# Query and key products of the second layer: three of four blocks as seven products on sums of pairs of weight tiles, with the sums made at the end of the first gated stage

## The chip, the core and the metric

The kernel runs on one core of a Trainium2 chip. The metric is the device time of one execution in microseconds (us); the time before is the median of three executions, 1891.64 us (1891.1 to 1893.27). The engines are named as in the profile: PE (TensorE matmul), PEld (its weight loads), DVE (VectorE), ACT (ScalarE), POOL (GpSimd) and SP (SyncE); POOL and SP issue most of the DMAs here, each in its program's order.

## The reference

Two layers, each an attention block and a gated block, with the same weights in both layers. S = 2048 tokens, D = 448, H = 16 heads of 28, F = 1792.

```python
def _A_ref(x, wqkv, wo):
    qkv = ((x @ wqkv).reshape(B, S, 3, H, Dh)).transpose(2, 0, 3, 1, 4)
    q, k, v = qkv[0], qkv[1], qkv[2]
    scores = jnp.einsum("bhqd,bhkd->bhqk", q, k) * (Dh ** -0.5)
    o = jnp.einsum("bhqk,bhkd->bhqd", softmax(scores), v)
    return o.transpose(0, 2, 1, 3).reshape(B, S, D) @ wo
def _B_ref(x, w_gate, w_up, w_down):
    return (sigmoid(x @ w_gate) * (x @ w_up)) @ w_down

x = x + _A_ref(layernorm(x), wqkv, wo)
x = x + _B_ref(layernorm(x), w_gate, w_up, w_down)
x = x + _A_ref(layernorm(x), wqkv, wo)
x = x + _B_ref(layernorm(x), w_gate, w_up, w_down)
```

## The kernel before

The tokens lie in 16 tiles of 128, worked on in four blocks of 512 (`NB = 4`, `W = 512`). All inputs of the matrix products are split into a high and a low float16 part, and three of the four part products are summed in PSUM (high by high, low by high, high by low). D = 448 is three tiles of 128 and a tail of 64; the tail's high and low parts share one tile.

Instructions stand on each engine in the order in which the code emits them (`tc.manual_schedule()`); there is no scheduler. SBUF is dealt out by two pools of slots, `big` (19 slots) and `qrt` (12): `get` takes the slot that has been free longest, `put` appends to the free list, and whoever writes a slot next waits for its last readers.

A layer is `project` (query, key and value products), `attend`, `out_project` and `gated`.

**project.** `qk(b, blk, fill, before)` makes the 896 query and key rows of one block as seven tiles of 128 rows. Each tile is one PSUM bank, 128 x 512, filled by `by_features` with 11 matmuls 512 wide (nine for the three whole tiles, two for the tail). ACT turns the bank into a high part (L765), DVE into a low part (L766), ACT squares (L768), DVE takes maxima of the squares (L772), the SP queue stores both parts in `qk_scr` (L775), and small matmuls (L744, L747) collect the squares of a head, three tiles late. `fill` holds work for the next block, done after the tile of that index. `vals` follows with four tiles of values of 11 matmuls 448 wide each (L587 to L592). After the last block, `guard_of_norms` pops the last collected norms (`fin`), loads the first heads, and bounds the scores; `attend` starts when the first score operands have landed.

**gated.** Gate and up products are already in the seven-product form, on pairs (128 x 256 quarters) of a weight pair: `of_halves` emits six 256-wide matmuls for the products 0 to 3 (operands `wide`) and five for 4 to 6 (operands `short`), and `gate_and_up` spreads the seven over a `chain` bank, which ACT copies out after each product, and a `side` bank, which DVE adds up. The sums of the weight tiles come from `Prepare`, which makes them once during the first layer's attention, with DVE alone, in float16 parts (`N_SUMS = 25` tiles of 128 x 128 a pair).

The down products lag one block behind: while block b does its gate and up products, `pieces` does the down products of block b - 1, one of the seven operand sets `dn` for each of the seven pairs p. After the last block a tail remains: the seven down products of block 3, in the order `TAIL = (0, 1, 3, 2, 5, 4, 6)`. The first three are run for six pairs each, then each is finished with the seventh pair; the other four follow whole, 42 matmuls of 224 columns each. `finish(b, k)` adds a bank to x on DVE (L1596), and products 2, 5 and 4 go on accumulating in the bank that the first three left, after that addition. `used_dn` gives the operand slot back and issues the load of the next operand set on the POOL queue, always three ahead:

```python
def used_dn(self):
    (big.put_next if self.pairs else big.put)(self.dn.popleft())
    if self.products:
        self.load_dn(nc.gpsimd)
```

During the last block of the first layer's gated stage, `steps` also holds the work for the first two blocks of the next layer (norms on DVE and POOL, `lift` on ACT, `square` on DVE, stores and gathers on SP), dealt out by `portions(b, p)`; and with the last pair `wq.load` brings the query, key and value parts back from `qk_parts` and `v_parts`, where the first layer had left them (`keep`).

Of the kernel before, what the change touches and what calls it, by code (L numbers as in the profile page):

```python
# [16 lines left out]
ALU = mybir.AluOpType  # L17
# [53 lines left out]
TAIL = (0, 1, 3, 2, 5, 4, 6)  # L71

# [46 lines left out]
def interleaved_layers(ctx: ExitStack, tc: tile.TileContext, x_in, wqkv, wo, w_gate, w_up,  # L119
# [122 lines left out]

    def powers(c, n, squares):
# [20 lines left out]
    class Block:  # L264
# [10 lines left out]
        def __init__(self, b, halves=False):  # L275
            self.b = b
            self.halves = halves
            self.turned = False
# [107 lines left out]
        def half_steps(self):  # L386
# [43 lines left out]
            def r11():  # L430
                self.wide = big.get("xwide", [P, 4, 2, 2, W // 2], F16)
                self.short = big.get("xshort", [P, 3, 2, 2, W // 2], F16)
# [36 lines left out]

            def last_low():  # L470
                low(self.short[:, 2], cut(2, 2))
# [7 lines left out]
            return [r11, t1, t2, t3, r21, t4, r22, last_low, last_rows]  # L479
# [121 lines left out]
    class WeightsQKV:  # L601
# [65 lines left out]

        def load(self):
            self.tiles()
            for i in range(2):  # L670
                nc.sync.dma_start(self.qk[i], qk_parts[i])
            nc.sync.dma_start(self.v, v_parts)

# [46 lines left out]
    def project(layer, wq, begun):  # L720
# [68 lines left out]

        def values_product(pv, blk, j, kts=range(4)):  # L790
            t = slice(j * P, (j + 1) * P)
            by_tokens(pv[:, 0:D], lambda kt: blk.hi[:, kt, t], lambda kt: blk.lo[:, kt, t],
                      blk.tail[:, t], wq.v, kts)

        def vals(b, blk, after, tiles=range(TB), at=None, begun=None):
            for j in tiles:
                pv = begun or bank(evac[0] % 4 if at is None else at, "vp")
                evac[0] += 1
# [31 lines left out]
        blks = begun + [Block(b) for b in range(len(begun), NB)]  # L830
# [3 lines left out]
        if layer == 0:  # L834
# [5 lines left out]
            def turned(kts):  # L840
                b1.turn_banks(6, kts)
                for j in range(TB):
# [9 lines left out]
                            3: lambda: (b2.squares(), b2.store(), tell.read())}  # L852
        else:
            ones_of_values()
            fill = [idle, lambda: b1.ready(0, 1), lambda: b1.ready(2, 3), b2.norm,
                    lambda: b2.squares([0, 1]), sq(2, 2, 3), b2.store]
            along_values = {0: b3.norm, 1: sq(3, 0, 1), 2: lambda: (fin(), b2.gather()),
                            3: sq(3, 2, 3)}
        fin = qk(0, blks[0], fill, None)
        vals(0, blks[0], along_values)  # L860
        if layer == 0:
            fill = [b2.gather, b3.norm, sq(3, 0, 1), sq(3, 2, 3), idle,
                    lambda: b2.ready(0, 1), lambda: (b2.ready(2, 3), b3.store())]
        else:
            fill = [idle, lambda: b2.ready(0, 1), lambda: b2.ready(2, 3), b3.store]
        fin = qk(1, b1, fill, None)
        vals(1, b1, {0: b3.gather, 2 if layer == 0 else 1: fin})
        add = tell.add if layer == 0 else idle
        fin = qk(2, b2, [idle, lambda: b3.ready(0, 1), lambda: b3.ready(2, 3), idle, add, add,
                         add], None)  # L870
        fin = qk(3, blks[3], [add, add, add], fin)
        if layer > 0:
            big.put(*wq.qk)
# [34 lines left out]
        vals(2, blks[2], {0: guard_of_norms, 3: worst_of_heads})  # L908
# [15 lines left out]
        def last_values(begun=None):  # L924
# [6 lines left out]
            if layer > 0:  # L931
                big.put(wq.v)
# [72 lines left out]
    class Prepare:  # L1005
# [86 lines left out]
        def add_up(self, v):  # L1092

            s12, s34 = [qrt.get("sums", [P, 2, 2, P]) for _ in range(2)]
            l11, l12, l21, l22 = v[:, 0:2, 0], v[:, 2:4, 0], v[:, 0:2, 1], v[:, 2:4, 1]
            for to, a, b, op in ((s12[:, 0], l21, l22, ALU.add),
                                 (s12[:, 1], s12[:, 0], l11, ALU.subtract),
                                 (s34[:, 0], l11, l21, ALU.subtract),
                                 (s34[:, 1], l12, s12[:, 1], ALU.subtract)):
                nc.vector.tensor_tensor(to, a, b, op=op)  # L1100
            return s12, s34

# [22 lines left out]
        def split(self, raw, kind, j):  # L1125
# [5 lines left out]
            elif kind in "gu":  # L1131
                m = "gu".index(kind)
                t = big.at(self.packs, "pack", [P, N_SUMS, P], F16)
                sums = self.add_up(v)
                s12, s34 = [a.rearrange("p a k n -> p (a k) n") for a in sums]
                for to, a in ((t[:, 0:2], v[:, 0:2, 0]), (t[:, 2:6], s12), (t[:, 6:10], s34),
                              (t[:, 10:14].rearrange("p (k z) n -> p k z n", k=2), v[:, 2:4])):
                    scaled_high(to, a, 4 + m, nc.vector)
                for to, hi, a in ((t[:, 14:16], t[:, 0:2], v[:, 0:2, 0]),
                                  (t[:, 16:20], t[:, 2:6], s12),  # L1140
                                  (t[:, 20:23], t[:, 6:9], s34[:, 0:3]),
                                  (t[:, 23:25], t[:, 10:12], v[:, 2])):
                    scaled_low(to, hi, a, 4 + m)
                scaled_low(t[64:P, 9], t[0:64, 9], s34[0:64, 3], 4 + m)
                scaled_low(t[64:P, 12:14], t[0:64, 12:14], v[0:64, 3], 4 + m)
# [785 lines left out]
```

## Time and profile before

| what | value |
|---|---|
| median of three executions | 1891.64 us |
| the profiled execution: time, and its span | 1891.53 us, 1889.8 us |
| PE, PEld busy | 1881.4 us (100%), 1334.4 us (71%) |
| DVE, ACT, POOL busy | 1444.7 us (76%), 1390.5 us (74%), 233.2 us (12%) |
| matmuls | 24,321 |
| DMA | 272 MB, mean 144 GB/s |
| first layer's gated stage, last down products (L1578) | 923.26 to 952.6 us |
| second layer's query, key and value products | 952.6 to 1052.7 us |
| the first of them: block 0 | query and key from 952.59, values from 969.49 us |

Times are counted from the start of the span. The time of an execution is 1.73 us longer than its span in the profiled run. A matmul's duration in the records includes its way through the array, which overlaps the next one; the step from one matmul to the next is read from two rows' starts divided by the matmuls between. In a timeline row, `x44` is the count of merged instructions, and a bracket gives the idle time of the engine ahead of it and what ended that.

### The profile page before, as it was taken

The page shows a single profiled execution, that of the slowest core. Times are in us where ns is not written, and L with a number is a line of the kernel's source. Part 1 is how long each engine was busy: PE and PEld are TensorE (multiplying, and loading weights), DVE is VectorE, ACT ScalarE, POOL GpSimd, SP SyncE. Part 2 cuts the span into 40 slices and gives each one's busy share as a digit, 9 for nine tenths or more (in the row PEclk, how much of TensorE's full clock was granted, in tenths as well). Part 3 has the DMA queues.
Part 4 walks back from the last instruction along what each step waited for, and adds up shares of the span by engine and source line. Part 5 has one row for each costly group of instructions (what it writes and reads, how often), then busy time and mean ns, then how long its engine had stood idle before and what let it go on. Part 6 is the DMA issues. An engine that isn't in the chain of part 4 may idle for free. (4 is left out here: it accounts for less than half of the span.)

```text
span 1889.8 us, 56477 instructions
## 1 busy us (share of the span) xinstructions
PE 1881.4 (100%) x24321; PEld 1334.4 (71%) x24321; DVE 1444.7 (76%) x2894; ACT 1390.5 (74%) x1793; POOL 233.2 (12%) x450
## 2 busy tenths in 40 slices
PE   9999999999999999999999999999999999999999
PEld 4455555556566899999954556766666568999998
DVE  7758989898977887787575487787778688877664
ACT  5569999999993655555345799999999747555541
POOL 3023112222102111111100000000000021111110
PEclk9999999999999999999999999999999999999999
DMA  7676444334323755646734322122120246566553
GB/s 247 194 217 162 133 132 128 106 121 132 101 89 93 261 207 208 228 180 243 251 97 134 90 52 50 30 52 52 30 49 21 72 160 234 200 227 223 207 207 142
DMA packets 109059, 272.01 MB, mean 144 GB/s; under 512 B 12958, under 2 KB 65566, under 8 KB 108672
## 3 DMA queue, kind: packets, MB, share of 16 engines
q0 software_dynamic: 32256, 160.12, 23.4%
q1 hardware_dynamic: 75392, 106.82, 19.8%
q8 instruction: 192, 3.15, 0.7%
q10 hardware_dynamic: 1152, 1.38, 0.3%
q14 instruction: 67, 0.55, 0.1%
HBM read 209.26 MB, written 50.62 MB: 138 GB/s over the span
## 5 line engine op out<-in xcount | busy, mean ns | idle before, releaser
L1233 ACT ACTIVATE prob_s<-sc 128x1536 f32<-128x1536 f32 (+1 forms) x657 | 888.0, 1485 | 7.3 <-DMA qp_s<-qk_scr 5.2
L1269 PE MATMUL acc<-prob_s,val_s 128*32 128x256 f32 (+3 forms) x7700 | 572.1, 384 | 0.0
L1218 PE MATMUL sc<-qp_s 114*32 114x512 f16 x7868 | 555.1, 379 | 0.0
L580 PEld LDWEIGHTS <-gu_s 128*128 128x128 f16 x4368 | 426.7, 98 | 46.1 <-PE op L1398 0.7
L1218 PEld LDWEIGHTS <-qp_s 114*32 114x32 f16 x8192 | 276.8, 95 | 200.4 <-issue 84.6
L1269 PEld LDWEIGHTS acc<-prob_s,val_s 128*32 128x32 f32 x7700 | 276.5, 110 | 139.7 <-issue 13.6
L580 PE MATMUL chain<-xwide_s,gu_s 128*128 128x256 f16 x2016 | 247.5, 273 | 0.1
L1578 PE MATMUL dnp<-dn_s,hparts_s 128*128 128x224 f16 x2184 | 245.9, 259 | 0.0
L1578 PEld LDWEIGHTS <-hparts_s 128*128 128x128 f16 x2184 | 210.2, 98 | 5.1
L1249 DVE SCALAR_TENSOR_TENSOR power_q<-power_q,expo_q 128x512 f32<-128x512 f32 x243 | 168.2, 692 | 8.3
L1651 ACT COPY one_q<-chain 128x256 f32<-128x256 f32 x224 | 82.4, 371 | 116.0 <-PE chain L580 115.5
L1667 DVE TENSOR_TENSOR one_q<-side,one_q 128x512 f32<-128x512 f32 x112 | 72.2, 686 | 99.0 <-PE side L580 98.6
L580 PE MATMUL side<-xshort_s,gu_s 128*128 128x256 f16 x1120 | 140.6, 273 | 0.0
L565 PE MATMUL qkp<-xhl_s,wqk_s 128*128 128x512 f16 x616 | 137.5, 379 | 0.9 <-ACT wqk_s L232 0.6
L1459 POOL DMA_DIRECT2D gu_s<-gu_parts x104 | 56.3, 541 | 428.4 <-PE side L580 424.9
L565 PEld LDWEIGHTS <-wqk_s 128*128 128x128 f16 x616 | 59.3, 98 | 70.1 <-ACT wqk_s L232 1.4
L1531 ACT CAST hparts_s<-hsums_q 128x256 f16<-128x256 f32 (+1 forms) x152 | 71.5, 485 | 37.1 <-DVE hsums_q L1543 23.4
L1298 DVE STREAM_TRANSPOSE oturned_q<-acc 128x512 f32<-128x512 f32 x32 | 22.9, 716 | 98.1 <-PE acc L1269 97.9
L1269 PE MATMUL acc<-power_q,val_s 128*32 128x256 f32 (+3 forms) x300 | 94.2, 396 | 0.0
L580 PE MATMUL side<-xwide_s,gu_s 128*128 128x256 f16 x672 | 91.7, 273 | 0.0
L765 ACT ACTIVATE qkhl_q<-qkp 128x512 f16<-128x512 f32 x56 | 33.2, 592 | 70.0 <-PE qkp L565 69.5
L1678 ACT ACTIVATE one_q<-one_q 128x512 f32<-128x512 f32 x56 | 35.3, 630 | 65.5 <-DVE one_q L1667 65.3
(215 smaller groups left out, 2283.8 us busy)
## 6 DMA issues: line engine op xcount, KB each, us to landing
gu_s<-gu_parts POOLq DMA_DIRECT2D x104, 800.0 KB, 5.9
dn_s<-dn_parts POOLq DMA_DIRECT2D x42, 784.0 KB, 7.5
qp_s<-qk_scr SPq DMA_DIRECT2D x96, 224.0 KB
qk_scr<-qkhl_q SPq DMA_DIRECT2D x56, 256.0 KB
gu_parts<-pack_s POOLq DMA_DIRECT2D x14, 800.0 KB, 3.8
xt_scr<-xs_s SPq DMA_DIRECT2D x48, 224.0 KB
xraw_s<-xt_scr SPq DMA_DIRECT2D x12, 768.0 KB
qp_s<-qk_scr SPq DMA_DIRECT2D x64, 112.0 KB
```

Of the source, the lines that this page charges most:

```text
L565: nc.tensor.matmul(pm, w, x, start=(i == 0), stop=(i == len(terms) - 1))
L580: nc.tensor.matmul(pm, a, x, start=(first and i == 0), stop=(i == len(terms) - 1), skip_group_check=True)
L1218: nc.tensor.matmul(ps[32 * j:32 * j + 32, :], hd.k[:, keys], hd.q[:, qb * W:(qb + 1) * W], start=True, stop=True, tile_position=(0, 32 * j))
L1233: nc.scalar.activation(prob[:, 0:n, :], ps[:, 0:n, :], AF.Exp, scale=exp_scale)
L1249: nc.vector.scalar_tensor_tensor(p, p, c[k], y, op0=ALU.add, op1=ALU.mult)
L1269: nc.tensor.matmul(acc[qb * VC:(qb + 1) * VC, s], v[:, kc % TB, h, :], probs[c * NB + qb][:, s], start=(kc == 0 and a == 0), stop=(kc == N ...
L1459: queue.dma_start(self.gu[-1][m], gu_parts[p, m])
L1531: nc.scalar.copy(to[:, :, 0], a)
L1578: nc.tensor.matmul(pm, a[:, x, t], w[:, p, y], start=(begin and n == 0 and (j == 0 or alone)), stop=(n == 2), skip_group_check=True)
L1651: nc.scalar.copy(to, pm)
L1667: nc.vector.tensor_tensor(one[m], side[m], one[m], op=ALU.add)
L1678: nc.scalar.activation(out, v, AF.Sigmoid, scale=gate_scale)
```

## The change

In the second layer, blocks 0, 2 and 3 no longer use `qk` but `qk_sums`; block 1 keeps `qk`. The seven row tiles are taken as three pairs, (0, 1), (4, 5), (2, 6), each in the seven-product form, and tile 3 alone in the usual form on 256-wide halves. A block then has 3 x 39 + 22 = 139 matmuls 256 wide in place of 77 matmuls 512 wide, and 16 norm matmuls 64 wide in place of 8 that are 128 wide. Each pair adds four ACT copies out of a chain bank and two DVE additions of a side bank, as in `gate_and_up`, ahead of the high, low and square steps of each tile. The operands of these blocks (`wide`, `short` with a fourth quarter) come from `half_steps` in place of `ready`, for value products as well.

The sums of the weight tiles are not kept from the first layer: `read_pairs` loads the six raw weight tiles again on the POOL queue (12 DMAs, after pair 5 of the last block), and `add_pair` makes the sums with `split_sums`: four DVE additions, four ACT high parts and six DVE low parts a pair. Pairs 0 and 1 are emitted after `finish(*done)`, ahead of the tail of down products; pair 2 with two more DVE multiplications after the fifth of them. The norms, lifts and transposes of block 2 (`third`) move into the tail too, in `go_on` after each down product. `wq.load` brings back only tile 3's parts and the value parts, and `load_usual` brings the whole query and key parts for block 1, at the start of `project`, on the POOL queue. `portions` deals out 32 steps instead of 24 in the last block, since block 0 needs ten half steps where it had two.

```diff
+PAIRS_QK = ((0, 1), (4, 5), (2, 6))
+ALONE = 3
...
+    def split_sums(t, v, by, engine=None):
...
+        sums = add_up(v)
+        s12, s34 = [a.rearrange("p a k n -> p (a k) n") for a in sums]
+        for to, a in ((t[:, 0:2], v[:, 0:2, 0]), (t[:, 2:6], s12), (t[:, 6:10], s34),
+                      (t[:, 10:14].rearrange("p (k z) n -> p k z n", k=2), v[:, 2:4])):
+            high(to, a)
...
+        low(t[64:P, 12:14], t[0:64, 12:14], v[0:64, 3])
...
+        def add_pair(self, j):
+            v, t = self.pair(j), big.get("wsums", [P, N_SUMS, P], F16)
...
+            split_sums(t, v, by)
+            if j > 0:
+                big.put(self.raws[j // 2])
...
+        def load_usual(self):
+            self.qk = [big.get("wqk", [P, 4, 2 * D], F16) for _ in range(2)]
+            for i in range(2):
+                nc.gpsimd.dma_start(self.qk[i], qk_parts[i])
...
+        def qk_sums(b, blk, points, before=None):
...
+            class Pair:
...
+                def on_chain(self, k, to):
+                    of_halves(self.chain[:, high], self.w, blk, k, k == 0)
+                    nc.scalar.copy(to, self.chain[:, high])
...
+                def c11_c22(self):
+                    of_halves(self.side[:, high], self.w, blk, 4, False)
+                    nc.vector.tensor_tensor(self.one, self.side, self.one, op=ALU.add)
...
+                def c12(self):
+                    of_halves(self.side[:, low], self.w, blk, 6, False)
+                    nc.vector.tensor_tensor(self.two[:, high], self.side[:, low],
+                                            self.two[:, high], op=ALU.add)
...
+            pa, pb = Pair(0, 0), Pair(1, 2)
+            pa.first()
+            pb.first()
+            at(0)
+            pa.apart()
+            pa.second()
+            pb.second()
...
+            pc.c21()
+            pc.tiles[0].high()
+            pc.tiles[0].low(pc.one)
+            lone.high()
+            lone.low()
+            pop()
+            pc.c12()
+            pc.tiles[1].high()
+            pc.tiles[1].low(pc.two)
+            pa.tiles[1].square()
+            pb.tiles[1].square()
+            lone.square()
+            pc.tiles[0].square()
+            pc.tiles[1].square()
...
+            fin = qk_sums(0, blks[0], {0: ready[0:1], 1: ready[1:2], 2: ready[2:3],
+                                       4: ready[3:4]})
+            vals(0, blks[0], {0: both(*h2[0:2]), 1: both(*h2[2:3], s3[0]),
+                              2: both(fin, h2[3]), 3: both(s3[1], h2[4])})
+            fin = qk(1, b1, [both(s3[2], s3[3], s3[6]), both(s3[4], s3[5], s3[7], s3[8]),
...
+            fin = qk_sums(2, b2, {0: h3[6:7], 1: h3[7:8], 2: h3[8:9], 4: h3[9:10]})
+            fin = qk_sums(3, b3, {}, fin)
...
-        vals(2, blks[2], {0: guard_of_norms, 3: worst_of_heads})
+        vals(2, blks[2], {layer: guard_of_norms, 3: worst_of_heads})
...
+            if b == NB - 1 and not last and p == NP - 2:
+                wq.read_pairs()
...
         finish(*done)
+        between = deque([[]] * NP)
+        if not last:
+            assert not steps
+            wq.load()
+            wq.add_pair(0)
+            wq.add_pair(1)
+            third = after[2]
+            turns = third.squared()
+            between = deque([turns[0:1], turns[1:2], turns[2:5] + turns[6:8],
+                             turns[5:6] + turns[8:] + [third.store],
+                             [third.gather, lambda: wq.add_pair(2)], []])
...
         for n in range(3):
             pieces(b, TAIL[n], [NP - 1], w[n])
             wt.used_dn()
             finish(b, TAIL[n])
+            go_on()
```

The change moves instructions in three places.

**The POOL queue at the end of the first gated stage.** `dn_s` is an operand set of a down product, `raws_s` the raw weight tiles, `rs` and `off` the norms of block 2; in brackets are the semaphores that an instruction waits for. Before, the last six loads of operand sets stand one behind the other:

```order
L1472 DMA dn_s_18202<-dn_parts 128x3136 [waits DMASW4_49,PE_49]
L1472 DMA dn_s_18376<-dn_parts 128x3136 [waits DMASW7_49,DMASW3_49,PE_49]
L1472 DMA dn_s_18508<-dn_parts 128x3136 [waits DMAHW1_49,DMAHW2_49,DMAHW0_49,DMAHW7_49,DMASW5_49,DVE_49]
L1472 DMA dn_s_18517<-dn_parts 128x3136 [waits DMASW6_49,PE_49]
L1472 DMA dn_s_18526<-dn_parts 128x3136
L1472 DMA dn_s_18572<-dn_parts 128x3136 [waits DMAHW6_49,DMAHW5_49,Activation_49]
```

Now:

```order
L1758 DMA dn_s_18427<-dn_parts 128x3136 [waits DMASW7_49,PE_49]
L1758 DMA dn_s_18596<-dn_parts 128x3136 [waits DMASW1_49,DMASW0_49,DMASW2_49,DVE_49,Activation_49]
L333 TENSOR_SCALAR rs_18600<-mv_18599 128x2 [waits DVE_49,Pool_49]
L335 TENSOR_TENSOR rs_18600<-rs_18600,nhalf 128x2 [waits Pool_49]
L344 TENSOR_TENSOR off_18609<-mv_18599,rs_18600 128x2 [waits Pool_49]
L346 TENSOR_SCALAR off_18609<-off_18609 128x2 [waits Pool_49]
L1758 DMA dn_s_18618<-dn_parts 128x3136 [waits PE_49]
```

The load for the fourth product of the tail (`dn_s_18596`) now takes the slot that `add_pair(1)` gave back, which held the raw tiles of pairs 0 and 1, so it waits for DVE and ACT to be done with them; the fifth and sixth stand behind the norms of block 2, which wait for DVE.

**DVE in the same place.** `x<-dnp` is the addition of a down product to x. Before, the additions of the tail follow the low parts of the last gated pair:

```order
L1535 TENSOR_TENSOR hparts_s_13729<-two_q_18210,hparts_s_13729 128x256
L1596 SCALAR_TENSOR_TENSOR x<-dnp_17156,back,x 128x2x224
L1596 SCALAR_TENSOR_TENSOR x<-dnp_18391,back,x 128x2x224
L1596 SCALAR_TENSOR_TENSOR x<-dnp_18428,back,x 128x2x224
L1596 SCALAR_TENSOR_TENSOR x<-dnp_18465,back,x 128x2x224
```

Now two pairs of sums (`sums_q`, `wsums_s`, ten rows each; the last seven of pair 1 are shown) stand between the first and the second of these:

```order
L254 TENSOR_TENSOR sums_q_18464<-raws_s_18234,sums_q_18463 128x256
L266 SCALAR_TENSOR_TENSOR wsums_s_18462<-raws_s_18234,up,wsums_s_18462 128x256
L266 SCALAR_TENSOR_TENSOR wsums_s_18462<-sums_q_18463,up,wsums_s_18462 128x512
L266 SCALAR_TENSOR_TENSOR wsums_s_18462<-sums_q_18464,up,wsums_s_18462 128x384
L266 SCALAR_TENSOR_TENSOR wsums_s_18462<-raws_s_18234,up,wsums_s_18462 128x256
L266 SCALAR_TENSOR_TENSOR wsums_s_18462<-sums_q_18464,up,wsums_s_18462 64x128
L266 SCALAR_TENSOR_TENSOR wsums_s_18462<-raws_s_18234,up,wsums_s_18462 64x256
L1882 SCALAR_TENSOR_TENSOR x<-dnp_18479,back,x 128x2x224
L329 BN_STATS st_0_18601<-x 128x6
L330 BN_AGGR mv_18599<-st_0_18601 128x2
```

The addition that frees the fourth product's bank now stands behind 20 DVE instructions on the sums, and is followed by the statistics of block 2.

**ACT between blocks 2 and 3 of the second layer's projections.** Before, a high part and a square alternate, tile by tile, through the end of block 2 and the start of block 3:

```order
L765 ACTIVATE qkhl_q_19298<-qkp_19285 128x512
L768 ACTIVATE sq_q_19299<-qkhl_q_19298 128x512
L765 ACTIVATE qkhl_q_19319<-qkp_19306 128x512
L768 ACTIVATE sq_q_19320<-qkhl_q_19319 128x512
L765 ACTIVATE qkhl_q_19340<-qkp_19327 128x512
L768 ACTIVATE sq_q_19341<-qkhl_q_19340 128x512
```

Now block 2 ends with a copy, three high parts and five squares, and the first copies of block 3 stand behind them:

```order
L956 COPY two_q_19634<-chain_19631 128x256
L917 ACTIVATE qkhl_q_19717<-one_q_19633 128x512
L917 ACTIVATE qkhl_q_19722<-alone_19630 128x512
L917 ACTIVATE qkhl_q_19735<-two_q_19634 128x512
L932 ACTIVATE sq_q_19740<-qkhl_q_19642 128x512
L932 ACTIVATE sq_q_19744<-qkhl_q_19667 128x512
L932 ACTIVATE sq_q_19748<-qkhl_q_19722 128x512
L932 ACTIVATE sq_q_19752<-qkhl_q_19717 128x512
L932 ACTIVATE sq_q_19756<-qkhl_q_19735 128x512
L956 COPY one_q_19763<-chain_19761 128x256
L956 COPY one_q_19767<-chain_19765 128x256
L956 COPY two_q_19764<-chain_19761 128x256
```

The copies `one_q<-chain` free the chain banks that block 3's second matmul group on each writes next; before, a tile had a bank to itself, and four banks took turns.

More of the change, by code (lines that the diff above doesn't have):

```diff
@@ L829, in project @@
                  nothing]
-        blks = begun + [Block(b) for b in range(len(begun), NB)]
+        blks = begun + [Block(b, layer == 1, True) for b in range(len(begun), NB)]
         idle = None
@@ L852, in project @@
                             3: lambda: (b2.squares(), b2.store(), tell.read())}
+        if layer == 0:
+            fin = qk(0, blks[0], fill, None)
+            vals(0, blks[0], along_values)
+            fill = [b2.gather, b3.norm, sq(3, 0, 1), sq(3, 2, 3), idle,
+                    lambda: b2.ready(0, 1), lambda: (b2.ready(2, 3), b3.store())]
+            fin = qk(1, b1, fill, None)
+            vals(1, b1, {0: b3.gather, 2: fin})
+            add = tell.add
+            fin = qk(2, b2, [idle, lambda: b3.ready(0, 1), lambda: b3.ready(2, 3), idle, add,
+                             add, add], None)
+            fin = qk(3, blks[3], [add, add, add], fin)
@@ L866, in project @@
[L866 to L871, printed above, removed]
+            wq.load_usual()
+            h2, h3, s3 = b2.half_steps(), b3.half_steps(), b3.squared()
+            ready = [lambda kt=kt: b1.ready(kt) for kt in range(4)]
@@ L872, in project @@
+            big.put(*wq.qk)
+            vals(1, b1, {0: h2[9], 1: both(fin, *h3[0:2]), 2: both(*h3[2:4]),
+                         3: both(*h3[4:6])}, banks=(3, 0, 2, 1))
+            fin = qk_sums(2, b2, {0: h3[6:7], 1: h3[7:8], 2: h3[8:9], 4: h3[9:10]})
+            fin = qk_sums(3, b3, {}, fin)
         if layer > 0:
-            big.put(*wq.qk)
+            big.put(*wq.sums)
+            evac[0] = 0
         else:
@@ L1483, in used_dn, with gated @@
                 self.load_dn(nc.gpsimd)
-    def gated(layer, first, wt, before_next):
+    def gated(layer, first, wt, wq):
         last = layer == LAYERS - 1
@@ L1789, in gated @@
                     wt.load_dn()
-            if b == NB - 1 and not last:
-                for f in (2 * p, 2 * p + 1):
-                    before_next(f)
+            if b == NB - 1 and not last and p == NP - 2:
+                wq.read_pairs()
         b = NB - 1
```

301 lines of the change are left out of this document (240 added, 61 removed).

## The prediction

> **What bounds the kernel now.** I read the page's totals first, then the windows around the change, then the timelines of PE, DVE, ACT and POOL there. The totals:
>
> ```profile
> span 1889.8 us, 56477 instructions
> PE 1881.4 (100%) x24321; PEld 1334.4 (71%) x24321; DVE 1444.7 (76%) x2894; ACT 1390.5 (74%) x1793; POOL 233.2 (12%) x450
> ```
>
> PE is busy for all but 8 us. The change takes a little work from PE and gives DVE and ACT more, so two questions decide: how many matmul steps go, and whether PE, which waits nowhere here, begins to wait. The windows over the end of the first gated stage (to 952.6 us) and the first half of the second layer's products show how much room the other engines have; the columns are busy time of PE, PEld, DVE, ACT and POOL, the granted clock, DMA share and GB/s:
>
> ```profile
> 920.00:940.00 20.00, 20.00 (x208) 19.77 (x207) 9.29 (x19) 3.49 (x7) 4.16 (x11) 1.00 0.95 322
> 960.00:980.00 20.00, 20.00 (x106) 9.84 (x105) 17.53 (x44) 9.24 (x16) 2.44 (x4) 1.00 0.39 113
> 980.00:1000.00 20.00, 20.00 (x104) 9.57 (x103) 14.62 (x37) 11.41 (x20) 0.00 (x0) 1.00 0.64 175
> ```
>
> PE is full in each. DVE has 10.7 us free in the first, only 2.5 and 5.4 us in the other two.
>
> **A. The work that PE saves.** A 256-wide and a 512-wide step, and a norm matmul:
>
> ```profile
> 907.97 1.25 PE L580 MATMUL chain<-xshort_s,gu_s 128*128 128x256 f16 x10
> 909.06 0.74 PE L1578 MATMUL dnp<-dn_s,hparts_s 128*128 128x224 f16 x6
> 975.73 0.33 PE L747 MATMUL knorm<-sq_q,ind 128*128 128x128 bf16 x3
> 977.98 9.66 PE L565 MATMUL qkp<-xhl_s,wqk_s 128*128 128x512 f16 x44
> 987.47 0.22 PE L744 MATMUL qnorm<-sq_q,ind 128*128 128x128 bf16 x1
> ```
>
> Ten 256-wide matmuls take 909.06 - 907.97 = 1.09, so 0.109 each; 44 that are 512 wide take 9.49, so 0.2157 each. A block goes from 77 x 0.2157 = 16.61 to 139 x 0.109 = 15.15. The norms were 8 at 0.055 (three in 0.33, of which a lone one has 0.22) = 0.44; 16 that are half as wide cost 0.44 to 0.88. So a block saves 1.0 to 1.5 us, and three blocks 3.0 to 4.4; I take 3.6. All of it is on the path, since PE is. That is the whole gain: 0.2% of the time, about what a measurement of this kernel can tell from no change.
>
> **B. A new wait in the tail of down products.** The fourth product's operands now land in the slot of the raw tiles of pairs 0 and 1. Their load, on the POOL queue, is released when DVE and ACT have made both pairs' sums. When PE wants it, and when DVE is done:
>
> ```profile
> 923.26 29.49 PE L1578 MATMUL dnp<-dn_s,hparts_s 128*128 128x224 f16 x306
> 952.59 9.66 PE L565 MATMUL qkp<-xhl_s,wqk_s 128*128 128x512 f16 x44
> ...
> 312.73 0.42 DVE L1100 TENSOR_TENSOR sums_q<-raws_s 128x256 f32<-128x256 f32 x1
> 314.20 0.35 DVE L230 TENSOR_SCALAR pack_s<-raws_s,up 128x256 f16<-128x256 f32 x1
> 315.65 0.48 DVE L235 SCALAR_TENSOR_TENSOR pack_s<-raws_s,up,pack_s 128x256 f16<-128x256 f32 x1
> 318.50 0.72 DVE L1298 STREAM_TRANSPOSE oturned_q<-acc 128x512 f32<-128x512 f32 x1
> 915.84 2.21 DVE L317 STREAM_TRANSPOSE xs_s<-lifted_q 128x448 f32<-128x448 f32 x4
> 927.37 0.68 DVE L1596 SCALAR_TENSOR_TENSOR x<-dnp,back,x 128x448 f32<-128x448 f32 x1
> ...
> DMA to landing us min/median/max: 4.5/7.1/20.6
> ```
>
> The step of a down matmul is (952.59 - 923.26) / 306 = 0.0958. Of these, 12 belong to the product before the tail and 3 x 42 = 126 to the tail's first three, so the fourth starts at 923.26 + 138 x 0.0958 = 936.5.
>
> DVE is done with the earlier block's addition at 927.37 + 0.68 = 928.05. Two transposes are moved behind the last pair, 2 x 0.55 = 1.1: 929.15. The same sums of one weight pair were made by DVE in the first layer: additions from 312.73 to 314.20, low parts from 315.65 to 318.50, together 4.3 (the high parts between them are ACT's now, and ACT was busy for 3.5 of 20 us here). Two pairs are 8.6: 937.75. The last row gives the operand loads' own time from issue to landing. They took 4.5 on a quiet queue and 7.1 in the median; here the load finds the queue idle, so 4.5: landed at 942.3, and PE waits 5.8. To the time of issue and the semaphores I give 0.4: **6.2**, with bounds of 5.0 (the sums a tenth shorter than the rows) and 8.4 (the median landing). Between the ends I take the quiet landing, since the earlier operands have long landed by then, and the raw tiles before their sums start.
>
> Behind it, the fifth load stands behind the norms of block 2 on the POOL queue, whose four steps ran as follows:
>
> ```profile
> 842.19 0.19 POOL L292 TENSOR_SCALAR rs<-mv 128x2 f32<-128x2 f32 x1 [4.57 <-DVE mv L289]
> 843.54 0.23 POOL L305 TENSOR_SCALAR off<-off 128x2 f32<-128x2 f32 x1
> 964.22 0.62 DVE L288 BATCH_NORM_STATS2 st<-x 128x6 f32<-128x448 f32 x1
> ```
>
> The addition of the tail's first product ends on DVE at 938.4, the statistics of its tiles some 1.4 later, the POOL steps (843.77 - 842.19 = 1.6) at 941.4; landed at 946. The fourth product then runs from 942.7 for 42 x 0.0958 = 4.0 and ends at 946.7, so this is hidden by 0.7; without B it would not be: PE would want it at 940.5 and wait some 5 us for it instead. The sixth and seventh loads have a product more of lead. The third pair's sums on DVE (4.3 and two multiplications) lie beside the last two products.
>
> **C. A wait between blocks 2 and 3.** A block's last pair ends with its evacuation, the high and low parts, and five squares in one piece on ACT; the next block's first copies stand behind them, and PE may not write a `chain` bank again before its copy.
>
> ```profile
> 955.16 0.60 ACT L765 ACTIVATE qkhl_q<-qkp 128x512 f16<-128x512 f32 x1 [28.84 <-PE qkp L565]
> 958.16 0.63 ACT L768 ACTIVATE sq_q<-qkhl_q 128x512 bf16<-128x512 f16 x1
> 958.70 1.12 ACT L219 CAST xhl_s<-xraw_s 128x512 f16<-128x512 f32 x2
> L1651 ACT COPY one_q<-chain 128x256 f32<-128x256 f32 x224 | 82.4, 371 | 116.0 <-PE chain L580 115.5
> L1674 DVE TENSOR_TENSOR two_q<-side,two_q 128x256 f32<-128x256 f32 x112 | 42.3, 418 | 0.0
> L766 DVE SCALAR_TENSOR_TENSOR qkhl_q<-qkp,qkhl_q 128x512 f16<-128x512 f32 x56 | 38.2, 682 | 29.6 <-ACT qkhl_q L765 29.5
> ```
>
> Let T be the end of block 2's last product on PE, five steps = 0.55 long. The `chain` product before it ends at T - 0.55; ACT copies it (0.37) and makes two high parts (2 x 0.6), which ends at about T + 1.1; DVE makes the low part of the lone tile (0.68, to T + 1.8) and only then adds the `side` bank (0.42, to T + 2.2); ACT makes the last high part (0.6, to T + 2.8), then five squares at 958.70 - 958.16 = 0.54 each (2.7, to T + 5.5), then the first copy (0.37): T + 5.9. PE meanwhile has two `chain` groups and one `side` group, 18 x 0.109 = 1.96. It waits 5.9 - 2.0 = 3.9; bounds 3.0 (each step overlaps the next by a tenth, as successive rows do) and 4.5. I take **3.8**.
>
> **D. A wait at the end of block 3.** The last five tiles' norms are popped by `fin` after the second value tile now. They need the same five squares and then two maxima each on DVE:
>
> ```profile
> 956.45 0.55 DVE L772 TENSOR_TENSOR sq_q<-sq_q 128x256 bf16<-128x256 bf16 x2
> 969.49 0.35 PE L590 MATMUL vp<-wv_s,xhl_s 128*128 128x448 f16 x1
> 969.68 0.35 PE L591 MATMUL vp<-wv_s,xhl_s 128*128 128x448 f16 x1
> ```
>
> The last is done at about T + 5.5 + 0.55 = T + 6; two value tiles cover 22 x 0.19 = 4.2. PE waits about 1.8 less what the pops do in between: **1.6**, bounds 0.5 and 2.5. The guard that follows still has six value tiles, 12.5 us, ahead of the first score.
>
> **E. DVE as a whole between 960 and 1000.** Operands of the seven-product form, and the additions of side banks:
>
> ```profile
> L1667 DVE TENSOR_TENSOR one_q<-side,one_q 128x512 f32<-128x512 f32 x112 | 72.2, 686 | 99.0 <-PE side L580 98.6 <-issue 0.2
> L404 DVE TENSOR_TENSOR t_q<-xraw_s 128x256 f32<-128x256 f32 x24 | 9.0, 416 | 0.0
> L423 DVE TENSOR_TENSOR xwide_s<-t_q,xwide_s 128x512 f16<-128x512 f32 x24 | 16.3, 680 | 0.0
> ```
>
> A block adds 3 x (0.69 + 0.42) = 3.3 us of additions, and its operands take 16 x 0.42 + 4 x 0.68 = 9.4 us where the usual form's four low parts took 2.7. DVE had 7.9 us free in these 40 us, and the next blocks' half steps put about 10 on it, so it runs full there and PE's evacuations come late now and then: I take **2.2** over blocks 0 and 2, bounds 0.5 and 5. This is the least certain term.
>
> **F. A slower restart of PE after B.** The opening of the kernel is the only place where PE starts after a long rest:
>
> ```profile
> 1.25 4.30 PE L262 MATMUL still<-still_q 128*128 128x512 f16 x13 [1.25 <-DVE warm L181]
> 7.98 0.66 PE L509 MATMUL turn<-ident,xn_s 128*128 128x128 f32 x4 [2.43 <-DVE xn_s L321]
> 8.47 0.38 PE L262 MATMUL still<-still_q 128*128 128x512 f16 x1
> 2.00:4.00 2.00, 2.00 (x6) 0.76 (x5) 0.00 (x0) 0.54 (x1) 0.00 (x0) 1.00 0.96 277
> ```
>
> Thirteen 512-wide matmuls took 4.30, where 12 x 0.2157 + 0.38 = 2.97 would do: 1.33 too much, with the clock column at 1.00 all the while. After a rest of 2.43 us the next 512-wide one had its usual 0.38. B's rest of 6 us is nearer to the opening; I take **1.3**, bounds 0 and 2.2.
>
> [...]
>
> **The sum.** -3.6 + 6.2 + 3.8 + 1.6 + 2.2 + 1.3 = +11.5. Against the profiled execution's 1891.53 (its median is 1891.64, 0.1 above, so nothing is added) that is **1903.0**. The first layer, the attention and the last gated stage keep their instructions, so nothing else is counted.
>
> **Rivals.**
>
> 1. *No slow restart*: B's wait costs only itself. For: the clock column never leaves 1.00. Against: the 1.33 of the opening. 1903.0 - 1.3 = 1901.7.
> 2. *Two slow restarts*: C's rest of 3.8 us, also longer than the 2.43 that did no harm, cools PE as well: 1903.0 + 1.3 = 1904.3. [...]
> 3. *A loaded queue and a full DVE*: the fourth load lands after the median 7.1 instead of 4.5 (+2.6 less the 0.4 given) and E is 3.5 instead of 2.2: +3.5, 1906.5. For: the window from 920 to 940 shows a DMA share of 0.95. Against: the raw tiles must have landed before the sums start.
> 4. *The other side, faster*: DVE and ACT work through the sums and squares at under half of the rows' durations, since these rows come from stages in which DVE had much else to do. The point from which it decides: B goes if both pairs take 2.8 us and not 8.6 (issue at 936.5 - 4.5 = 932.0), C if its chain takes 2.0 and not 5.9. Then A alone remains, 1887.9. Against it: the rows of a single instruction are the same, 0.42, in the attention and in the gated stage.
> 5. *Nothing to tell*: B at a third, C and D halved, no E and F: -3.6 + 2.1 + 1.9 + 0.8 = +1.2, 1892.7. It needs all of these at once.
>
> **Chances.** Forecast 0.46, rival 1 0.22, rival 2 0.10, rival 3 0.14, rival 4 0.04, rival 5 0.04. The likeliest is the forecast, 1903.0. The range takes in the first four cases with B at 5.0 and E at 0.5 below (1903.0 - 1.3 - 1.2 - 1.7 - 1.3 of C, D and A = 1897.5) and rival 3 with A at 3.0 and C at 4.5 above (1906.5 + 1.3 = 1907.8); I take 1897 to 1909. Slower by over 0.2% (3.8 us) 0.92, within it 0.04, faster 0.04.
>
> **What would show it.** In the changed profile: a gap on PE of about 6 us ahead of the fourth product of the tail, ended by a landing of `dn_s`, whose issue on the POOL queue comes right after the last low part of pair 1 on DVE; a gap of almost 4 us in block 3's second `chain` group, ended by ACT's copy behind five squares; gaps of about half a microsecond between the norm matmuls that follow the second value tile of block 2; DVE near full from 965 to 1000. The forecast is wrong if PE shows no gap of over 2 us before the first score, if 139 matmuls and their norms don't take 15.6 to 16.0 us where nothing waits, or if the stages before 923 or after the first score differ.

## The result, and the profile after

The changed kernel takes 1911.29 us (median of five, 1908.9 to 1912.49) where the kernel before takes 1892.11 (five runs, 1891.1 to 1893.27): a ratio of 1.010, with a 95% interval of 1.0085 to 1.0114. It is slower, as forecast, but by 19 us and not by 11.5, and it lies above the range. The profiled execution took 1910.08 us, 18.55 more than that of before.

The totals of the page of the changed kernel, and PE's waits from 900 to 1080 us in its trace (total, times, longest; the same view of the kernel before is empty):

```profile
span 1908.4 us, 57171 instructions
PE 1884.7 (99%) x24531; PEld 1364.3 (71%) x24531; DVE 1478.9 (77%) x2984; ACT 1425.9 (75%) x1885; POOL 250.5 (13%) x482
...
PE dnp L1864 <- DMA dn_s<-dn_parts: 8.0, 1, 8.0
PE chain L633 <- ACT one_q L956: 3.3, 1, 3.3
PE chain L633 <- ACT val_s L1102: 1.6, 1, 1.6
PE norms L899 <- DVE sq_q L936: 0.9, 4, 0.3
PE side L633 <- ACT val_s L1102: 0.7, 1, 0.7
PE side L633 <- DVE one_q L972: 0.7, 2, 0.4
PE sc L1504 <- DMA qp_s<-g_scr: 0.7, 1, 0.7
```

These are 15.9 us of waits. The list counts a wait from the modelled end of the matmul before, so each costs some 0.16 us more from start to start (a down matmul's record lasts 0.259 us, its step 0.0958). The other large item is not a wait. The windows around the two long ones (PE busy, granted clock, DMA share, GB/s):

```profile
937.00:941.00 4.00, 0.19 (x2) 0.98 1.14 238
941.00:945.00 4.00, 0.00 (x0) 0.50 1.01 415
945.00:951.00 6.00, 5.83 (x32) 0.50 0.61 245
951.00:955.00 4.00, 4.00 (x43) 0.99 0.26 69
...
1040.00:1043.00 3.00, 3.00 (x24) 0.50 0.02 5
```

The clock is at half from 941 on, in the middle of the wait, and stays there for six microseconds after PE has started again; it falls again after the wait of 3.3 us. PE's rows at the same places:

```profile
923.80 13.39 PE L1864 MATMUL dnp<-dn_s,hparts_s 128*128 128x224 f16 x138
945.17 19.14 PE L1864 MATMUL dnp<-dn_s,hparts_s 128*128 128x224 f16 x168 [7.97 <-DMA dn_s<-dn_parts]
964.14 1.52 PE L633 MATMUL chain<-xwide_s,wsums_s 128*128 128x256 f16 x12
...
1034.43 0.82 PE L633 MATMUL side<-xwide_s,wsums_s 128*128 128x256 f16 x6
1038.53 1.50 PE L633 MATMUL chain<-xwide_s,wsums_s 128*128 128x256 f16 x12 [3.28 <-ACT one_q L956]
1041.64 2.26 PE L633 MATMUL chain<-xwide_s,wsums_s 128*128 128x256 f16 x12
```

138 matmuls of the down products pass before the wait and 168 after it, as forecast. The 168 take 964.14 - 945.17 = 18.97 us, where 168 x 0.0958 = 16.1 would do: the half clock costs 2.9. Twelve 256-wide matmuls at 1041.64 have 2.26 where the twelve at 1038.53 have 1.50.

From the first output projection to the layer's first score, the stretch that holds the whole change, the kernel before takes 486.9 us (565.80 to 1052.70) and the changed one 505.5 (566.34 to 1071.87): +18.6, which is all of the difference. Within it the tail (from the 138 matmuls at 923.80 to the first query and key product) takes 40.3 us where it took 29.3.

### The profile page after: what moved, and what is told of

Same layout as the page of the kernel before. It is cut to its first block, busy times and chain, and to the rows that moved or that the text cites. A ratio compares the mean times of both kernels' runs of the same rounds, so it can differ in the third digit from the quotient of the medians.

```text
span 1908.4 us, 57171 instructions
## 1 busy us (share of the span) xinstructions
PE 1884.7 (99%) x24531; PEld 1364.3 (71%) x24531; DVE 1478.9 (77%) x2984; ACT 1425.9 (75%) x1885; POOL 250.5 (13%) x482
## 5 line engine op out<-in xcount | busy, mean ns | idle before, releaser
L1555 PEld LDWEIGHTS acc<-prob_s,val_s 128*32 128x32 f32 x7700 | 282.0, 110 | 130.3 <-issue 12.8
L618 PE MATMUL qkp<-xhl_s,wqk_s 128*128 128x512 f16 x385 | 86.5, 379 | 0.9 <-ACT wqk_s L235 0.6
L1529 DVE TENSOR_SCALAR expo_q<-aside,base 128x512 f32<-128x512 f32 x81 | 60.6, 748 | 22.5 <-PE aside L1504 22.3
L1821 DVE TENSOR_TENSOR hparts_s<-hsums_q,hparts_s 128x256 f16<-128x256 f32 (+1 forms) x152 | 72.5, 516 | 5.8 <-ACT hparts_s L1817 5.8
```

The lines of the kernel that those rows point to most:

```text
L618: nc.tensor.matmul(pm, w, x, start=(i == 0), stop=(i == len(terms) - 1))
L1529: nc.vector.tensor_scalar(y, ps, base2[:, 0:1], -126.0, op0=ALU.mult, op1=ALU.max)
L1555: nc.tensor.matmul(acc[qb * VC:(qb + 1) * VC, s], v[:, kc % TB, h, :], probs[c * NB + qb][:, s], start=(kc == 0 and a == 0), stop=(kc == N ...
L1821: nc.vector.tensor_tensor(to[:, :, 1], a, to[:, :, 0], op=ALU.subtract)
```

## The experiments

Each is an edit of the changed kernel. The kernel before ran beside them at 1892.7 to 1892.9 us (1892.1 beside the changed kernel); the changed kernel was not run again, so a difference of 1 us to its 1911.3 says little. Comments in the code shown here are not in the kernels. Where a time is given for a part of the stage, it is from the start of one part on PE to that of the next, in the profiled execution.

**Is the slow stretch after a wait due to PE's rest?** PE's waits are filled with matmuls into an unused bank, whose results nobody reads:

```diff
+        pm, a = bank(7, "still"), store[0][:, 0]
+        for i in range(34):                       # t8_warm_longer: 42
+            nc.tensor.matmul(pm, a[:, 0, 0:P], a, start=(i == 0), stop=(i == 33))
         for k in TAIL[3:]:
...
             pa.apart()
+            if b == 3:
+                # 26 matmuls 256 wide into bank 6
             pa.second()
```

> The changed kernel with idle PE time filled, and nothing else: 34 matmuls 512 wide (7.3 us) into an unused bank ahead of the tail's fourth down product, 26 that are 256 wide (2.8 us) ahead of block 3's second copied product. The waits themselves stay. Theory: PE's clock falls to half after a wait of 3 us or more, and the two slow restarts cost 2.9 us (168 down matmuls in 18.97 instead of 16.10) and 1.9 us; kept busy, PE stays at full clock, so about 1911.3 - 4.8 = 1906.5. Rival: the slow stretch after the wait is the operands' or the DMA's doing (DMA share 1.0 there), or the added matmuls only push the rest back: 1911 to 1913, and 168 down matmuls again take 19 us.

It took 1910.71 us (1908.62 to 1913.6). The operands landed later in the profiled run, so that a rest of 2.0 us was left, and the clock fell all the same; PE's row and the windows around it:

```profile
948.07 17.93 PE L1869 MATMUL dnp<-dn_s,hparts_s 128*128 128x224 f16 x168 [2.04 <-DMA dn_s<-dn_parts]
...
946.00:948.00 2.00, 0.03 (x1) 1.00 0.98 319
949.00:952.00 3.00, 3.00 (x18) 0.50 0.52 217
```

This told nothing on the first wait, and I repeated it with more matmuls. Behind the second filler the clock stayed at 1.00, but in this execution it fell at block 2's start, after waits of 1.7 and 0.75 us: it was at 0.50 from 1020.44 to 1023.85.

> As t1_warm with 42 idle-time matmuls (9.1 us) ahead of the fourth product where 34 left a rest of 2.0 us, after which the clock still fell. Theory: no rest over 1 us is left there, the clock stays at 1.00, the 168 down matmuls take 16.1 us, and the tail takes 38.4 us or less where it took 40.3: about 1911.3 - 1.9 - 1.9 = 1907.5. Rival (the clock falls for another reason, such as the DMA load at that time): they take 18 to 19 us again, and the whole 1911 or more.

1909.31 us (1907.56 to 1910.99). The row and the windows:

```profile
947.92 16.27 PE L1869 MATMUL dnp<-dn_s,hparts_s 128*128 128x224 f16 x168 [0.21 <-DMA dn_s<-dn_parts]
...
948.00:953.00 5.00, 5.00 (x53) 1.00 0.48 194
1040.00:1044.00 4.00, 4.00 (x47) 1.00 0.00 0
```

Behind this rest of 0.21 us the clock stayed at 1.00, and the 168 take 16.1 us from start to start, at the same place as in t1_warm and beside much the same load (DMA shares of 0.48 and 0.52). The stretch from the output projection to the first score is 3.1 us shorter (502.45), of which 1.6 in the tail, though the operands came later than in the changed kernel, and 1.6 in blocks 2 and 3. So in these runs the half clock went with PE's rest (2.04 us against 0.21) and not with the load; the rival falls. The median came down by 2.0, about half of the 3.8 that were forecast, and the ranges of the two kernels overlap.

**The wait of 8 us.** The fourth product's operands get a slot that is free:

```diff
+            wt.load_dn(nc.gpsimd)      # in the slot of wv
             wq.load()                  # without wv
             wq.add_pair(0)
             wq.add_pair(1)
+            wq.load_v()                # in the slot of the raw tiles
...
-            wt.used_dn()
+            wt.used_dn(last or n < 2)
```

> The changed kernel, with the operands of the tail's fourth product loaded ahead of the sums into a slot that was free (that of the value parts), and the value parts into the raw tiles' slot behind the sums; the fifth and sixth loads then go one step earlier. Order on DVE as before. Theory: the wait of 8.1 us goes with its slow restart of 2.9 us; what is late next is DVE's addition of the first tail product, behind the sums, 1 to 2 us: 1911.3 - 11.0 + 1.5 = about 1902. Rival: the load only moves the wait to the fifth product (behind the norms on the POOL queue) or to the value parts: 1906 to 1911.

1902.49 us (1901.81 to 1904.86): 8.8 less. The tail takes 33.4 us where it took 40.3. What is late next, from PE's waits:

```profile
PE dnp L1866 <- DVE x L1884: 1.7, 1, 1.7
PE dnp L1866 <- DMA dn_s<-dn_parts: 1.7, 1, 1.7
```

The first is the one that was named, DVE's addition behind the sums; the second is a load that stands behind the norms on the POOL queue. Both rests are short, and the clock stayed at 1.00 behind them.

The next kernel also moves DVE's work in the tail:

```diff
             wq.add_pair(0)
-            wq.add_pair(1)
...
-            between = deque([turns[0:1], turns[1:2], turns[2:5] + turns[6:8], ...
+            between = deque([[lambda: wq.add_pair(1), wq.load_v], turns[0:1], turns[1:2],
+                             turns[2:5] + turns[6:8], [lambda: wq.add_pair(2)], ...
```

Unlike t2_slot it also loads an operand set after the tail's third product (`wt.used_dn()` stays as it was in the changed kernel).

> As t2_slot, and in the tail the sums of pair 1 and the norms of block 2 one product later each, pair 2's sums one earlier, so that neither DVE's additions nor the norms on the POOL queue stand ahead of what the down products need. Theory: the tail takes 29.3 to 30.2 us as in the kernel before (t2_slot still had two waits of 1.7), and the whole is 1911.3 - 11.0 + 0.5 = about 1901. Rival: DVE's work in the tail doesn't fit beside it in any order, and 2 us or more of waits stay: over 1903.

1902.63 us (1901.19 to 1905.53), no better than t2_slot: the tail is 31.7 us, 1.7 less, but three waits of 0.5 to 0.7 us stay in it, the longest of them for a load that still stands behind the norms on the POOL queue (issued at 946.49, landed at 952.01). The time lies between the two theories; the gain of the tail does not show in the median.

**Why the load took longer than the rows of before.** The load of the value parts leaves the SP queue:

```diff
-            nc.sync.dma_start(self.v, v_parts)
...
-            between = deque([turns[0:1], turns[1:2], turns[2:5] + turns[6:8], ...
+            between = deque([turns[0:1], turns[1:2],
+                             [lambda: nc.gpsimd.dma_start(wq.v, v_parts)] + turns[2:5] + ...
```

> The changed kernel, with the 896 KB load of the value parts issued on the POOL queue behind the tail's sixth load, not on the SP queue at the moment when the fourth load runs. Theory: the fourth load then lands in 4.6 us and not 6.4, the wait is 6.3 and not 8.1, the slow restart stays: about 1911.3 - 1.8 = 1909.5. Rival: the load is slow for another reason, and it still takes over 6 us: 1911.

DVE, POOL and SP queue in the changed kernel's timelines, its operand loads' time to landing between 920 and 960 us, and the same of the experiment with PE's row there:

```profile
937.69 0.47 DVE L266 SCALAR_TENSOR_TENSOR wsums_s<-raws_s,up,wsums_s 64x256 f16<-64x256 f32 x1
938.71 0.53 POOL L1758 DMA_DIRECT2D dn_s<-dn_parts  x1 [14.42 <-DVE wsums_s L266]
939.00 0.34 SPq L746 DMA_DIRECT2D wv_s<-v_parts  x1
DMA to landing us min/median/max: 4.5/5.3/6.4
...
DMA to landing us min/median/max: 4.5/4.8/5.4
944.25 18.72 PE L1863 MATMUL dnp<-dn_s,hparts_s 128*128 128x224 f16 x168 [6.39 <-DVE xs_s L358]
```

The load was issued where it was forecast, and took the longest of the five in that stretch, 6.4 us (from 938.7 to 945.1, just before PE starts). The value parts' load went out 0.3 us behind it. Without that neighbour the load takes 4.8 us (939.37 to 944.21; the transpose in the bracket only ended at about the same time), the wait is 6.39 (expected 6.3), and the tail 2.0 us shorter (38.3). The whole did not follow: 1911.65 us (1909.81 to 1912.16). In the profiled run blocks 2 and 3 take 42.3 us instead of 39.3: there the clock also fell after the short waits at block 2's start, which it did not do in the changed kernel and which costs 1.7, and the half clock after the wait between the blocks lasted longer (2.8 us lost, not 1.65). A window of each:

```profile
1018.00:1019.00 1.00, 1.00 (x7) 0.50 0.00 0
1040.00:1042.00 2.00, 2.00 (x17) 0.50 0.04 8
```

So the cause of the longer landing is shown in the tail of one execution each, and no gain in the time is.

**The wait between blocks 2 and 3.** Block 2's last parts and squares are emitted one at a time behind block 3's first six products:

```diff
-            pc.tiles[1].high()
-            pc.tiles[1].low(pc.two)
-            pa.tiles[1].square()
...
+            rest = deque([lambda: (pc.tiles[1].high(), pc.tiles[1].low(pc.two)),
+                          pa.tiles[1].square, pb.tiles[1].square, lone.square, ...
+            if b != 2:
+                while rest:
+                    rest.popleft()()
...
             pa.first()
+            behind()                   # before.rest.popleft()(), also behind the next five
```

> The changed kernel, with block 2's last high and low part and its five squares emitted one by one behind block 3's first six copies, and its last norms two groups later. Theory: the wait of 3.3 us between the blocks goes but for some 0.3, and with it the slow restart of 1.9: 1911.3 - 4.9 = about 1906.4. Rival: ACT and DVE have no room in block 3 either, and the wait comes back at the next copies: 1909 to 1911.

1906.0 us (1903.37 to 1909.27), as the theory had it. Blocks 2 and 3 take 34.4 us and not 39.3: the wait of 3.3 is gone from the list, and with it the half clock.

**The waits at block 2's start.**

```diff
-                if j in after:
+                if j in after and not then:
                     after[j]()
...
+                if j in after and then:
+                    after[j]()
...
-                         3: both(*h3[4:6])}, banks=(3, 0, 2, 1))
+                         3: both(*h3[4:6])}, banks=(3, 0, 2, 1), then=True)
```

> The changed kernel, with block 1's value copies emitted ahead of the half steps of block 3 that follow each value tile, not behind them. Theory: the waits of 1.6 and 0.75 us at block 2's start, where the matmul banks wait for value copies that stand on ACT behind half steps whose raw tiles landed late, go but for some 0.4: 1911.3 - 1.9 = about 1909.4. Rival: the half steps come late instead and block 2 or 3 waits for its operands: 1911 to 1912.

1909.38 us (1907.73 to 1910.77). The number was met, within the spread of both kernels, but not by the mechanism: the two waits of 1.6 and 0.75 us became 1.1 and 0.6, since copies and half steps still share ACT. Where they came from, in ACT's timeline of the changed kernel:

```profile
1012.47 0.71 ACT L453 CAST xwide_s<-xraw_s 128x256 f16<-128x256 f32 x2 [3.29 <-DMA xraw_s<-xt_scr]
1013.79 0.54 ACT L1102 ACTIVATE val_s<-vp 128x448 f32<-128x448 f32 x1
```

ACT waits 3.3 us for block 3's raw tiles with the value copy behind them. Blocks 2 and 3 take 37.0 us and not 39.3, and the rest of that gain is that the clock did not fall after the 3.3 us wait, which is unchanged in this kernel; PE's row and the windows:

```profile
1040.68 1.47 PE L633 MATMUL chain<-xwide_s,wsums_s 128*128 128x256 f16 x12 [3.28 <-ACT one_q L956]
1054.39 1.30 PE L1084 MATMUL vp<-wv_s,xwide_s 128*128 128x448 f16 x6
...
1040.00:1042.00 2.00, 1.32 (x13) 1.00 0.50 137
1042.00:1044.00 2.00, 2.00 (x28) 1.00 0.00 0
```

From the end of that wait to the values it takes 1054.39 - 1040.68 = 13.7 us; in the changed kernel 1038.53 to 1053.89, 15.4. So the second slow restart cost 1.65 in that execution. It is not a fixed price: after the same wait of 3.28 us this stretch takes 16.6 us in t2_slot, a loss of 2.9.

**All cures together.**

> All cures together: t5_tail (pair 1's additions ahead of the first tail addition, its low parts behind), t3_squares, t4_copy_first, block 3's squares of the second tiles one step earlier, and a block's two norm pops one group later. Theory: what the change saves on PE is 1.0 to 1.5 us a block, 3.0 to 4.4 in all, and waits of some 0.3 to 0.6 us stay at six places: about 1891, between 1889 and 1893, the same as the kernel before. Rival: the waits move on to places not yet seen, and it stays at 1895 or more.

1897.38 us (eleven runs, 1894.86 to 1901.14), ratio to the kernel before 1.0022 (1.0013 to 1.0032): 14 us less than the change, but over the 1893 expected. Waits of 6.1 us stay:

```profile
PE dnp L1888 <- DMA dn_s<-dn_parts: 1.8, 1, 1.8
PE side L637 <- DVE one_q L980: 1.6, 3, 0.6
PE side L637 <- ACT val_s L1124: 0.9, 1, 0.9
PE sc L1528 <- DMA qp_s<-g_scr: 0.8, 1, 0.8
PE chain L637 <- ACT one_q L964: 0.6, 1, 0.6
PE chain L637 <- DVE x L1906: 0.4, 1, 0.4
```

> t7_all, with the value parts' load on the POOL queue behind the tail's last operand load (in t7_all it ran beside the fifth's, which took 9.6 us to land), and block 3's half steps after value tiles 2 and 3 one step later. Theory: the tail goes from 32.0 to about 30, block 2's start loses 1.3 us of waits, and the whole is 1897.4 - 3.3 = about 1894; the kernel before stays ahead, since what is left of small waits (0.3 to 0.8 us at each block's end and at the first score) eats the 3.4 us that PE saves. Rival 1: below 1890.7, the saving shows. Rival 2: 1897, the waits move once more.

1896.04 us (eleven runs, 1892.79 to 1898.81), ratio 1.0013 (1.0004 to 1.0022): between the theory and the second rival. Block 2's start lost 1.3 us of waits as expected (blocks 2 and 3: 32.75 us, and 33.96 in the kernel before). The tail did not gain: it takes 33.9 us where t7_all's takes 32.0. PE's wait of 2.15 us ended with the first of two operand loads that go out together (938.00 to 944.98, 7.0 us); the second, issued 0.6 us behind it, took 10.0, and PE did not wait for it. In t7_all too the load that PE waited for took 6.7 us (936.65 to 943.29), and the 9.6 are of the one behind it. The value parts' load was out of the way here (issued at 947.91), so the reason of these landings stays open. With that wait the clock fell:

```profile
945.03 13.82 PE L1887 MATMUL dnp<-dn_s,hparts_s 128*128 128x224 f16 x126 [2.15 <-DMA dn_s<-dn_parts]
945.00:946.00 1.00, 0.97 (x6) 0.50 1.00 357
```

The recorded mean of the granted clock parts these runs: the six of t10_all with a mean of 1.000 took 1892.79 to 1896.04 us (median 1894.0), the five with 0.998 or 0.999 took 1897.0 to 1898.81. So the forecast of 1894 holds for the executions that kept the clock, and they are no faster than the kernel before (1892.86). No version tried beats the kernel before.

## Why the prediction was right or wrong

| step | forecast | measured in the changed kernel |
|---|---|---|
| A, work saved on PE | -3.6 | about -3.3 (from t3_squares: blocks 2 and 3 take 34.36 with 2.6 of waits, so 31.7 against 33.96, 1.1 a block) |
| B, wait in the tail | 6.2 | 8.0 |
| C, wait between blocks 2 and 3 | 3.8 | 3.3 |
| D, wait at the end of block 3 | 1.6 | 0.9 in the list, 1.6 from start to start (below) |
| E, smaller waits of blocks 0 and 2 | 2.2 | 1.6 + 0.7 + 0.7 = 3.0 |
| F, slow restart | 1.3, once | 4.55: 2.9 after B, 1.65 after C |
| first score | 0 | 0.7 |
| sum (D as in the list) | +11.5 | +17.2 of +18.6 |

**Right**: which way it went, and where. The waits of B, C and D are in the trace, with the releaser that was named; of E's, only those of 0.36 us that DVE ends. The steps of B up to the issue hold to a fraction: DVE was forecast to be done at 937.75 and the row ends at 938.2, on a trace that runs 0.54 later; the fifth load, behind the norms, is hidden as forecast.

**Wrong: F, by 3.3 us.** The step that failed took the opening's 1.33 us as the price of a slow restart, with 2.2 as its upper bound, and counted it once. The loss after B was 2.9, since the clock came back only at 951.09, six microseconds after PE had started, and C cost a second restart, 1.65, with the clock at 0.50 from 1039.84 to 1043.25. The opening's row was no price: the record of the clock in that trace begins at 3.96, so the column's 1.00 ahead of it says nothing; the 512-wide matmuls step by 0.43 us up to there and by 0.22 behind it, and the 1.33 is half of those 2.7 us. In the changed kernel and in t2_slot the same thirteen matmuls took 5.11 and 5.73 us. The price differed from run to run (last section): after a rest of 7.6 us in t3_squares the clock was back some 2.6 us after PE had started, and the restart cost 1.3; that the term's number came true there is chance. The second restart stood as rival 2 with 0.10, at the same 1.3. What came true was that rival at a higher price together with the late landing of rival 3; the range had taken the rivals one at a time.

**Wrong: the landing in B, by 1.8.** The quiet 4.5 us was chosen for the reason that the earlier operands and the raw tiles would have landed. The order of the SP queue was not read for that time: the value parts' load goes out 0.3 us behind this one. t9_values_late shows it.

**A little low: E and the first score**, 0.8 and 0.7. The two longer waits in block 2, 2.3 of E's 3.0, are not DVE's fullness, as argued, but ACT's: value copies stand behind half steps whose raw tiles land late. DVE was not near full from 965 to 1000 either: it was busy for 27.0 of these 35 us, and for 27.3 in the kernel before. The six value tiles were taken to cover the guard, and they miss by 0.7.

The 1.4 us of the 18.6 that no row has are mostly in how the list counts. From start to start, B is 8.15 (923.80 + 138 x 0.0958 = 937.02, to 945.17), C 3.4, E 3.7, the first score 0.9, and A by the same count -4.1. D is 1.6, as forecast: the twelve norm matmuls take from 1058.05 to 1060.04 = 1.99 where twelve of them take 0.35 in block 0 (986.79 to 987.14). With F that makes 18.3.

## What to carry to other kernels

On an engine that is busy all the time, a saving of a few microseconds is worth only what its new waits leave, and here the granted clock sometimes fell to 0.50 behind them: a wait of 3.28 us cost nothing more in t4_copy_first, 1.65 in the changed kernel and 2.9 in t2_slot, and the wait of 8.0 in the changed kernel 2.9. When a buffer is given to new work, ask who takes its slot next and what its load stands behind, and read every queue at that moment, not only the one that is changed. When a saving is no larger than the sum of the small waits around it (some 3 to 4 us here, against the 6.1 us of waits that t7_all still had), curing the large ones does not bring it in.

## What the hardware did that I had not expected

How long a rest makes the clock fall was not one number in these traces: a rest of 2.04 us was followed by half clock (t1_warm), and 3.28 us was not (t4_copy_first), though the same 3.28 us in the changed kernel was. In t9_values_late waits of 1.8 and 0.75 us close together were enough, and in t1_warm 1.7 and 0.75; in the changed kernel 1.6 and 0.75 were not. In the changed kernel a half clock also began after PE had started again, at 1039.84 for a wait that ended at 1038.53.

How long the half clock went on was not one number either. In the changed kernel the granted clock was 0.50 from 940.85 to 951.09, with PE at work for 5.9 us of that, and from 1039.84 to 1043.25, all of it with PE at work. The rows (PE busy, granted clock, DMA share, GB/s) are windows around the tail's wait of 7.63 us in t3_squares, which ended at 945.00, and around the wait of 3.28 us between blocks 2 and 3 in t2_slot, which ended at 1031.98:

```profile
940.00:945.00 5.00, 0.01 (x1) 0.58 0.92 352
945.00:950.00 5.00, 5.00 (x39) 0.74 0.83 291
...
1028.00:1032.00 4.00, 0.72 (x8) 0.89 0.59 167
1032.00:1035.00 3.00, 3.00 (x22) 0.50 0.17 45
1035.00:1038.00 3.00, 3.00 (x20) 0.51 0.00 0
```

By the mean clock of these windows, full clock was back at about 947.6 in t3_squares, 2.6 us after PE had started, and at about 1037.9 in t2_slot, 6 us after. In each of these cases the loss (2.9 and 1.65 in the changed kernel, 1.3, 2.9) is about half of the time that PE worked at 0.50 (5.9 and 3.4, 2.6, 6). No experiment moved a rest alone, so what decides whether the clock falls behind one, and when it comes back, is not shown here.
